# Attention, then two MLPs, on one core: four of the first MLP's sixteen FF chunks, instead of five, run along with the attention

## The chip, the core and the metric

One core of a Trainium2 chip runs the whole program. The metric is the device time of one execution in microseconds (us), as the median of several runs. TensorE (PE in the profile) multiplies, VectorE (DVE), ScalarE (ACT) and GpSimd (POOL) do the elementwise work, and SyncE's queue (SP) issues the DMAs. The weight loads of TensorE are listed as PEld.

## What is computed

Three stages follow one another on 4 x 576 = 2304 tokens. An attention with 8 heads of 64 (causal softmax, plus a memory term that is mixed in with a gate) gives x with 512 columns; the first MLP and the second MLP follow:

```python
a = softmax(causal(q @ k.T / 8)); local = a @ v
x = g * mem_out + (1 - g) * local              # (2304, 512)
h = x @ w_in                                   # w_in 512 x 2048
r = maximum(h, 0)
x = (s * (r * r) + b) @ w_out                  # w_out 2048 x 512
h = x @ w2_in; e = exp(h - h.max(-1))          # w2_in 512 x 1024
solu = h * e / e.sum(-1)
out = layernorm(solu) * g_ln @ w2_out          # w2_out 1024 x 512
```

All of it is float32 at the interface. The weights come as 64-bit numbers and are decoded on the chip.

## The kernel before, in words

A framework places the instructions: the program gives an order, a list scheduler with a simulated timeline puts the instructions on each engine's queue when it holds them to be ready, earlier program order first, and each engine then runs its queue strictly in that order. So an instruction can be put ahead of others that come before it in the program, unless an explicit edge (`tc.issue_after(ins)`, for instructions on the engine of `ins`) or a tile that isn't free yet holds it back.

**Precision.** Every matmul of the MLPs is a sum of three: the operands are split in a high and a low part, and high x high, high x low and low x high are added up in PSUM. `split_x` (L440) does this for x in 4 ACT and 4 DVE instructions (L442, L443).

**Weights.** `decode(n)` (L141) loads the n-th weight tile of a list `order` (512 KB, L147) and turns it into a high and a low float32 part: two ACT instructions (L152, L163), five DVE instructions (L153, L154, L156, L158, L164) and one POOL instruction (L159). `decode_to(n)` (L175) decodes up to the n-th tile; its ACT instructions are put behind the instruction in `mark`. Pool A holds RA tiles and pool B, which takes the attention's memory once that is free, RB; RA + RB is 25, and the list has 48 tiles.

**Attention.** `Attention` (L188) goes over 16 units (4 sequences x 4 pairs of heads). Each unit has five score steps, followed by transposes and the product with the values; the unit's part of x is written by L411. Sequence by sequence, x also goes to DRAM (`xd`, L414).

**First part of the first MLP.** The 2048 hidden columns are 16 chunks of 128. The first FP1 = 5 chunks are worked off sequence by sequence in `first_part` (L447), as a filler among the attention's instructions: for each half sequence of 288 tokens, FP1 hidden steps (`hidden`, L420: 12 matmuls of 288 columns, L424 to L426, then ACT L427, DVE L434, ACT L435, DVE L438) and 4 output steps (15 matmuls of 288 columns, L471 to L473, an ACT copy L475 and a store to `yd`, L477). Fillers start in the second sequence; a counter `debt` (L554) sets how many filler steps stand behind each score step. What is left when the attention has ended is worked off in a loop of its own (L567); there each step asks for one more weight tile, up to 25. This stretch is called the handoff here.

**Second part.** `second_part` (L571) takes the other FP2 = 11 chunks in two groups (5 and 6), each over five blocks of tokens (four of 512 and one of 256): a round is one group on one block. A round loads its block of x (L493), splits it, and does for each chunk a hidden step (12 matmuls, then four ACT instructions L427, L429, L430, L431 and one DVE, L432) and an output step (12 matmuls, L608 to L610). Four PSUM banks add up the round's outputs, which are added to `yT` (L638). The first round's split is put behind the last ACT copy of the first part (`lastact`, L588). Further weight tiles are decoded along the way.

**Second MLP.** `mlp2` (L685) goes over 18 tiles of 128 tokens. The first tile's softmax is begun in the last round, with its three statistics in three small tiles of their own (L630).

The lines that the change touches:

Of the kernel before, what the change touches and what calls it, by code (L numbers as in the profile page):

```python
# [8 lines left out]
F32 = mybir.dt.float32  # L9
# [8 lines left out]
P = 128  # L18
# [5 lines left out]
def attention_mlp_kernel(  # L24
# [9 lines left out]
    nc = tc.nc  # L34
# [60 lines left out]
        with nc.allow_non_contiguous_dma(reason="a small vector"):  # L95
            nc.sync.dma_start(gl_sb, g_ln.rearrange("(f p) -> p f", p=P))

    FP1 = 5
    FP2 = NF - FP1
    RA = 2 * FP1 + 8  # L100
    RB = 25 - RA
    assert 2 * FP2 <= RA + RB
    wpA = ctx.enter_context(tc.tile_pool(name="wpA", bufs=RA))
# [71 lines left out]
    def decode_to(n):  # L175
        while decoded[0] < min(n, NW):
            with tc.issue_after(mark[0]) if mark[0] else nullcontext():
                decode(decoded[0])
            decoded[0] += 1
# [235 lines left out]


    attended = [False]
    lastact = [None]

    def hidden(w, xh, xl, n, ps, r, gh, gl, square=False):  # L420

# [18 lines left out]
    def split_x(x, xh, xl):  # L440
        for c in range(NC):
            nc.scalar.activation(xh[:, c], x[:, c], AF.Copy)  # L442
            nc.vector.tensor_tensor(xl[:, c], x[:, c], xh[:, c].bitcast(F32), ALU.subtract)  # L443
# [3 lines left out]
    def first_part(b, pools):  # L447

        xs, gs, ys, _ = pools
        for sub in range(2):  # L450
            nm = f"{b}_{sub}"
            x = xbs[b][:, :, sub * N1:(sub + 1) * N1]
            xh = xs.tile([P, NC, N1], F32R, tag="xh", name=f"xh{nm}")
            xl = xs.tile([P, NC, N1], F32R, tag="xl", name=f"xl{nm}")
            split_x(x, xh, xl)
            gq = []
            for f in range(FP1):
                ps = pools[3][0].tile([P, 512], F32, tag="mh"[len(pools[3]) - 1], name=f"h{nm}_{f}")
                r = gs.tile([P, N1], F32, tag="r", name=f"r{nm}_{f}", bufs=2)
                g = gs.tile([P, 2, N1], F32R, tag="g", name=f"g{nm}_{f}")  # L460
                decode_to(f + 1)
                hidden(wtiles["in", f], xh, xl, N1, ps[:, 0:N1], r, g[:, 0], g[:, 1])
                gq.append(g)
                yield
            for c in range(NC):
                ps = pools[3][-1].tile([P, 512], F32, tag="m", name=f"y{nm}_{c}")
                o = ps[:, 0:N1]
                decode_to(2 * FP1)
                for f in range(FP1):
                    wc = [wtiles["out", f][:, t, c * P:(c + 1) * P] for t in range(2)]  # L470
                    nc.tensor.matmul(o, wc[0], gq[f][:, 0], start=(f == 0), stop=False)  # L471
                    nc.tensor.matmul(o, wc[1], gq[f][:, 0], start=False, stop=False)
                    nc.tensor.matmul(o, wc[0], gq[f][:, 1], start=False, stop=(f == FP1 - 1))  # L473
                y = ys.tile([P, N1], F32, tag="y", name=f"yo{nm}_{c}")
                lastact[0] = nc.scalar.activation(y, o, AF.Copy).ins  # L475
                t0 = b * S + sub * N1
                nc.sync.dma_start(yd[:, c, t0:t0 + N1], y)  # L477
                yield
# [19 lines left out]
    with ExitStack() as fctx:  # L498
        xp = fctx.enter_context(tc.tile_pool(name="xp", bufs=2))
        xs = fctx.enter_context(tc.tile_pool(name="xs", bufs=1))  # L500
        gs = fctx.enter_context(tc.tile_pool(name="gs", bufs=FP1 + 1))
        ys = fctx.enter_context(tc.tile_pool(name="ys", bufs=2))
        ps_m = fctx.enter_context(tc.tile_pool(name="ps_m", bufs=2, space=PSUM))
        fpools = [xs, gs, ys, [ps_m]]
        filler = []
        with ExitStack() as actx:
            at = Attention(actx, xp)
            NS = CF + 1
            G = NU * NS
            at.load(0, "kq")  # L510
            warm_up(16)
            load_gate()
            at.load(1, "kq")
            at.load(0, "q", "z", "v")
            at.phi(0)
            at.load(1, "q", "v")
            load_consts()
            LAG = 2
            FG = NPAIR * NS + LAG + 1
            debt = 0.0  # L520
            tiles_of = lambda i: (2 * i, 2 * i + 1) if i < CF else (2 * CF,)
            for g in range(G + LAG):
                u, i = divmod(g, NS)
                if g < G and i != 1:
                    at.scores(u, *((0, 1) if i == 0 else (i,)))
                if g < 4:
                    with tc.issue_after(at.last):
                        warm_up(6)
                if i == CF and u < NU:
                    at.load(u + 2, "kq")  # L530
                if i == 3 and u < NU:
                    at.load(u + 2, "q")
                    at.load(u + 1, "z")
                if i == 2 and 0 < u < NU:
                    at.phi(u)
                if i == 3 and u < NU:
                    at.gates(u)
                if i == CF and u < NU:
                    at.weigh(u)
                if 0 <= g - LAG:  # L540
                    lu, li = divmod(g - LAG, NS)
                    for t in tiles_of(li):
                        at.transposes(lu, t)
                    if li == CF - 1:
                        at.recip_t(lu)
                        at.phi_t(lu)
                    if li == CF:
                        at.values(lu)
                        at.load(lu + 2, "v")
                        if lu % NPAIR == NPAIR - 1:  # L550
                            filler.append(first_part(lu // NPAIR, fpools))
                decode_to(min(int(g / 3.4), RA))
                if filler and g >= FG:
                    debt += 0.93 * 6 * (FP1 + NC) / (G - FG)  # L554
                    while debt >= 1 and filler:
                        debt -= 1
                        if next(filler[0], 0) == 0:
                            filler.pop(0)
        wpools[1] = ctx.enter_context(tc.tile_pool(name="wpB", bufs=RB, side="right", reuse_waits="tile"))
        xs2 = pctx.enter_context(tc.tile_pool(name="xs2", bufs=1, side="right", reuse_waits="tile"))  # L560
        gs2 = pctx.enter_context(tc.tile_pool(name="gs2", bufs=2, side="right", reuse_waits="tile"))
        ps_y = pctx.enter_context(tc.tile_pool(name="ps_y", bufs=1, side="right", space=PSUM, reuse_waits="tile"))
        ps_h = pctx.enter_context(tc.tile_pool(name="ps_h", bufs=2, side="right", space=PSUM, reuse_waits="tile"))
        fpools[3] = [ps_h, ps_m]
        load2(0, False)
        attended[0] = True
        for it in filler:  # L567
            for _ in it:
                decode_to(min(decoded[0] + 1, RA + RB))

    def second_part():  # L571
        load2(0, True)
# [4 lines left out]
        for ri, (fs, bi) in enumerate(rounds):  # L577
# [7 lines left out]
            x = xq.pop(ri)  # L585
            xh = xs2.tile([P, NC, NB], F32R, tag="xh", name=f"xh2_{ri}")
            xl = xs2.tile([P, NC, NB], F32R, tag="xl", name=f"xl2_{ri}")
            with tc.issue_after(lastact[0]) if ri == 0 else nullcontext():  # L588
                split_x(x[:, :, 0:n], xh[:, :, 0:n], xl[:, :, 0:n])
            ys = [ps_y.tile([P, 512], F32, tag=f"y{c}", name=f"y2_{ri}_{c}") for c in range(NC)]  # L590
            gq = {}

# [19 lines left out]
            for i, f in enumerate(fs):  # L612
                hstep(f)
                if i >= 1:
                    ystep(fs[i - 1])
                step += 1
                if ri == 0:
                    decode_to(min(decoded[0] + 2, g2))
                elif ri < len(blocks):

                    decode_to(g2 + (late - g2) * step // steps)
                elif ri < last:

                    decode_to(late + (last2 - late) * step // steps)
                else:
                    decode_to(decoded[0] + 1)
                if ri == last and i == 2:

                    z = dec.tile([P, WN, 2], I32, tag="raw", name="z0").rearrange("p n t -> p (n t)").bitcast(F32)
                    first["z"] = weights_of(0, z, *(const.tile([P, 1], F32, name=f"t0_{k}") for k in range(3)))  # L630
            if ri == last:
                decode_to(NW)
                first[1] = products(1)
# [36 lines left out]
    def weights_of(t, z, mx, sm, mu):  # L670

        hh = products(t) if t not in first else first.pop(t)
        nc.vector.tensor_reduce(mx, hh, AX.X, ALU.max, negate=True)
        nc.scalar.activation(z, hh, AF.Exp, bias=mx, accum_out=sm)
        nc.vector.tensor_scalar(sm, sm, 1e-9, None, ALU.add)
        nc.vector.reciprocal(sm, sm)
        nc.vector.scalar_tensor_tensor(z, hh, sm, z, ALU.mult, ALU.mult, accum_out=mu)
        return z, mu
# [119 lines left out]
```

## Time and profile before

| | us |
|---|---|
| median of three runs | 884.39 |
| lowest and highest run | 883.9, 886.73 |
| the profiled execution | 885.48 |
| its span, first to last instruction | 883.7 |
| TensorE busy in it | 850.8 (96%) |
| VectorE, ScalarE, GpSimd busy in it | 539.9, 513.7, 182.8 |

The profile shows one execution. An engine's busy time is the union of its instructions; for TensorE the end of a matmul is modelled and overlaps the next one's start, so the rate of work is read from the distance of starts, not from durations. "Idle before" is the time an engine stood still ahead of an instruction, with the instruction that ended it.

### The profile page before, as it was taken

How to read it: one execution, taken by the hardware profiler on the slowest of the kernel's cores; microseconds unless marked ns; L12 is line 12 of the kernel's file. 1: busy time of each engine (PE TensorE's matmuls, PEld its weight loads, DVE VectorE, ACT ScalarE, POOL GpSimd, SP SyncE). 2: the span in 40 equal slices, each digit the busy share in tenths (PEclk: the TensorE clock that was granted, in tenths of full speed). 3: DMA queues.
4: the chain of work that ended last, by engine and by line, in shares of the span. 5: the costliest groups of instructions: out<-in, count | busy, mean ns of one | idle time of the engine just before them, and what ended most of it. 6: DMA issues, size and time to landing. Idle time of an engine off the chain costs nothing.

```text
span 883.7 us, 14245 instructions
## 1 busy us (share of the span) xinstructions
PE 850.8 (96%) x5344; PEld 699.0 (79%) x5344; DVE 539.9 (61%) x1236; ACT 513.7 (58%) x1094; POOL 182.8 (21%) x180
## 2 busy tenths in 40 slices
PE   7899889999999999899999999999999999999997
PEld 5677668888878878878888888888988888888885
DVE  3898986768778467922338864454775444454532
ACT  4776765666666665555558776556774333433332
POOL 4445351332333222200002311101120000000000
PEclk9999999999999999999999999999999999999999
DMA  7445242533343204472013422111200000000000
GB/s 228 133 148 184 79 155 59 155 97 119 115 149 118 69 1 156 147 263 95 3 45 114 144 100 96 48 48 55 89 24 1 25 25 23 13 24 24 25 25 36
DMA packets 41494, 76.44 MB, mean 86 GB/s; under 512 B 6352, under 2 KB 20176, under 8 KB 41424
## 3 DMA queue, kind: packets, MB, share of 16 engines
q1 hardware_dynamic: 41424, 75.52, 26.5%
q8 instruction: 42, 0.69, 0.3%
q14 instruction: 28, 0.23, 0.1%
HBM read 61.35 MB, written 14.16 MB: 85 GB/s over the span
## 4 chain that ended last, share of the span: by engine, by line
PE 78%; DVE 13%; ACT 3%; issue 2%; POOL 1%; DMA 1%; POOLq 0%; SPq 0%; ACTq 0%; DVEq 0%
PE h L424 7%; PE h L425 7%; PE h L426 7%; PE y L609 5%; PE y L608 5%; PE y L610 5%; PE h L665 4%; PE h L666 4%; PE h L667 4%; PE o L730 4%; PE o L729 4%; PE o L728 4%; PE pp L372 3%; PE s L315 3%; PE po L404 3%
## 5 line engine op out<-in xcount | busy, mean ns | idle before, releaser
L425 PE MATMUL h<-xl,w 128*128 128x512 f32 (+2 forms) x380 | 131.0, 345 | 2.1 <-DVE xl L443 2.1
L159 POOL TENSOR_TENSOR wa<-wa,raw 128x512 f32<-128x512 f32 x48 | 67.8, 1415 | 314.5 <-DVE raw L158 198.2
L424 PE MATMUL h<-xh,w 128*128 128x512 f32 (+2 forms) x380 | 130.0, 349 | 2.8 <-ACT xh L442 2.5
L426 PE MATMUL h<-xh,w 128*128 128x512 f32 (+2 forms) x380 | 129.2, 341 | 0.0
L427 ACT ACTIVATE r<-h 128x512 f32<-128x512 f32 (+2 forms) x95 | 45.6, 489 | 87.3 <-PE h L426 73.0
L298 ACT ACTIVATE pr<-pr,mx 128x128 f32<-128x128 f32 (+3 forms) x128 | 70.8, 555 | 37.5 <-DVE mx L331 37.5
L432 DVE TENSOR_TENSOR gl<-r,gh 128x512 fp32r<-128x512 f32 (+1 forms) x55 | 37.2, 685 | 88.1 <-ACT r L431 88.0
L424 PEld LDWEIGHTS h<-xh,w 128*128 128x128 f32 x380 | 70.9, 188 | 15.2 <-ACT xh L442 3.5
L425 PEld LDWEIGHTS h<-xl,w 128*128 128x128 f32 x380 | 71.5, 188 | 13.1 <-DVE xl L443 3.8
L608 PE MATMUL y<-gh,w 128*128 128x512 f32 (+1 forms) x220 | 80.8, 372 | 0.0
L609 PE MATMUL y<-gh,w 128*128 128x512 f32 (+1 forms) x220 | 80.8, 372 | 0.0
L426 PEld LDWEIGHTS h<-xh,w 128*128 128x128 f32 x380 | 71.5, 188 | 8.1 <-issue 0.4
L331 DVE CUSTOM_DVE_ANT_0 pr<-s,big 128x128 f32<-128x128 f32 (+3 forms) x128 | 56.2, 485 | 9.6 <-PE s L315 9.2
L375 ACT ACTIVATE pt<-pp 128x256 f32<-128x256 f32 (+2 forms) x96 | 47.2, 518 | 22.5 <-PE pp L372 22.0
L610 PE MATMUL y<-gl,w 128*128 128x512 f32 (+1 forms) x220 | 60.0, 372 | 0.0
L728 PE MATMUL o<-w,zh 128*128 128x512 f32 x144 | 56.8, 395 | 0.8 <-ACT zh L722 0.8
L730 PE MATMUL o<-w,zl 128*128 128x512 f32 x144 | 56.9, 395 | 0.6 <-DVE zl L723 0.6
L667 PE MATMUL h<-w,yl 128*128 128x512 f32 x144 | 56.6, 393 | 0.0
L729 PE MATMUL o<-w,zh 128*128 128x512 f32 x144 | 56.6, 393 | 0.0
L665 PE MATMUL h<-w,yh 128*128 128x512 f32 x144 | 56.6, 393 | 0.0
L666 PE MATMUL h<-w,yh 128*128 128x512 f32 x144 | 56.6, 393 | 0.0
L315 PEld LDWEIGHTS s<-kq 64*128 64x128 f32 x640 | 40.1, 187 | 19.3 <-issue 6.7
(142 smaller groups left out, 1959.1 us busy)
## 6 DMA issues: line engine op xcount, KB each, us to landing
raw<-in_moe_w_in_dram SPq DMA_DIRECT2D x24, 512.0 KB, 3.8
raw<-in_moe_w_out_dram SPq DMA_DIRECT2D x24, 512.0 KB, 3.5
kq<-in_kq_dram SPq DMA_DIRECT2D x16, 608.0 KB, 4.0
xr<-xd SPq DMA_DIRECT2D x8, 1024.0 KB, 5.9
q<-in_q_dram SPq DMA_DIRECT2D x16, 320.0 KB, 3.0
v<-in_v_dram SPq DMA_DIRECT2D x16, 320.0 KB, 3.1
xd<-xb SPq DMA_DIRECT2D x4, 1152.0 KB, 6.5
yd<-yo SPq DMA_DIRECT2D x32, 144.0 KB, 2.4
```

The lines of the kernel that those rows point to most:

```text
L424: nc.tensor.matmul(ps, wc[0], xh[:, c, 0:n], start=(c == 0), stop=False)
L425: nc.tensor.matmul(ps, wc[0], xl[:, c, 0:n], start=False, stop=False)
L426: nc.tensor.matmul(ps, wc[1], xh[:, c, 0:n], start=False, stop=(c == NC - 1))
L608: nc.tensor.matmul(o, wc[0], gh[:, 0:n], start=(f == fs[0]), stop=False)
L609: nc.tensor.matmul(o, wc[1], gh[:, 0:n], start=False, stop=False)
L610: nc.tensor.matmul(o, wc[0], gl[:, 0:n], start=False, stop=(f == fs[-1]))
L665: nc.tensor.matmul(o, yh[:, c], w[:, 0], start=(c == 0), stop=False)
L666: nc.tensor.matmul(o, yh[:, c], w[:, 1], start=False, stop=False)
L667: nc.tensor.matmul(o, yl[:, c], w[:, 0], start=False, stop=(c == NC - 1))
L728: nc.tensor.matmul(oo, zh, w[:, 0], start=(f == 0), stop=False)
L729: nc.tensor.matmul(oo, zh, w[:, 1], start=False, stop=False)
L730: nc.tensor.matmul(oo, zl, w[:, 0], start=False, stop=(f == NF2 - 1))
```

## The change

It moves one of the five chunks of the first part into the second, which then has twelve in two groups of six. It also drops the edge that holds the first round's split behind the last copy of the first part, lets the loop after the attention ask for a weight tile at every fourth step only (and the first rounds for the rest, evenly), and keeps the three statistics of the second MLP's first tile in columns of an older constant. Pool A keeps 18 tiles and pool B 7.

```diff
-    FP1 = 5
+    FP1 = 4
     FP2 = NF - FP1
-    RA = 2 * FP1 + 8
+    RA = 2 * FP1 + 10
     RB = 25 - RA
...
-    lastact = [None]
...
-                lastact[0] = nc.scalar.activation(y, o, AF.Copy).ins
+                nc.scalar.activation(y, o, AF.Copy)
...
         attended[0] = True
+        turn = 0
         for it in filler:
             for _ in it:
-                decode_to(min(decoded[0] + 1, RA + RB))
+                turn += 1
+                decode_to(min(decoded[0] + (turn % 4 == 0), RA + RB))
...
-            with tc.issue_after(lastact[0]) if ri == 0 else nullcontext():
-                split_x(x[:, :, 0:n], xh[:, :, 0:n], xl[:, :, 0:n])
+            split_x(x[:, :, 0:n], xh[:, :, 0:n], xl[:, :, 0:n])
...
                 if ri == 0:
-                    decode_to(min(decoded[0] + 2, g2))
+                    decode_to(decoded[0] + step % 2)
+                    early = decoded[0]
                 elif ri < len(blocks):
 
-                    decode_to(g2 + (late - g2) * step // steps)
+                    decode_to(early + (late - early) * step // steps)
...
-                    first["z"] = weights_of(0, z, *(const.tile([P, 1], F32, name=f"t0_{k}") for k in range(3)))
+                    first["z"] = weights_of(0, z, *(gate[:, k:k + 1] for k in range(3)))
```

## Rows read from the trace of the kernel before

**Rows 1.** Windows: stretch, us, PE, PEld, DVE, ACT, POOL busy, PEclk, DMA, GB/s.

```profile
119.00:322.70 203.70, 200.73 (x1696) 166.72 (x1695) 143.84 (x412) 133.00 (x349) 68.55 (x65) 1.00 0.35 108
...
337.10:384.50 47.40, 42.56 (x290) 39.94 (x290) 37.93 (x66) 24.33 (x57) 10.98 (x7) 0.96 0.52 161
384.50:676.00 291.50, 290.19 (x1375) 240.01 (x1376) 156.75 (x262) 186.96 (x315) 33.25 (x23) 1.00 0.25 82
```

**Rows 2.** Timeline, DVE: L411 ends units 1, 4, 6 and 15. Start, us.

```profile
29.05 0.69 DVE L411 TENSOR_TENSOR xb<-po,R 128x512 f32<-128x512 f32 x1
...
75.25 0.69 DVE L411 TENSOR_TENSOR xb<-po,R 128x512 f32<-128x512 f32 x1
...
119.02 0.69 DVE L411 TENSOR_TENSOR xb<-po,R 128x512 f32<-128x512 f32 x1
...
322.74 0.69 DVE L411 TENSOR_TENSOR xb<-po,R 128x512 f32<-128x512 f32 x1
```

**Rows 3.** Windows of L424 alone, then of L471 alone: stretch, us, PE busy.

```profile
119.00:322.70 203.70, 30.51 (x96) 17.96 (x96) 1.00 0.35 108
...
119.00:322.70 203.70, 31.49 (x102) 19.17 (x102) 1.00 0.35 108
```

**Rows 4.** Groups by line on PE from 337.1 to 384.5 us.

```profile
L471 PE MATMUL y<-g,w 128*128 128x288 f32 x52 | 16.0, 310 | 1.3 <-ACT g L435 1.1 <-ACT yo L475 0.3
...
L424 PE MATMUL h<-xh,w 128*128 128x288 f32 x44 | 13.0, 304 | 0.8 <-ACT xh L442 0.8
```

**Rows 5.** Timeline, PE: first and last of 18 back-to-back matmuls of 288 columns.

```profile
349.04 0.29 PE L471 MATMUL y<-g,w 128*128 128x288 f32 x1
...
351.29 0.29 PE L473 MATMUL y<-g,w 128*128 128x288 f32 x1
```

**Rows 6.** Timeline, PE: first and last of 23 back-to-back matmuls of 512 columns.

```profile
391.62 0.40 PE L425 MATMUL h<-xl,w 128*128 128x512 f32 x1
...
396.78 0.40 PE L426 MATMUL h<-xh,w 128*128 128x512 f32 x1
```

**Rows 7.** Timeline, PE, handoff: matmuls that waited, with the wait and what ended it.

```profile
357.78 0.40 PE L425 MATMUL h<-xl,w 128*128 128x288 f32 x1 [1.40 <-DVE xl L443]
...
374.52 0.53 PE L473 MATMUL y<-g,w 128*128 128x288 f32 x2 [0.42 <-DVE g L438]
376.12 0.52 PE L471 MATMUL y<-g,w 128*128 128x288 f32 x1 [1.07 <-ACT g L435]
...
379.56 0.43 PE L471 MATMUL y<-g,w 128*128 128x288 f32 x1 [0.26 <-ACT yo L475]
...
384.92 0.74 PE L424 MATMUL h<-xh,w 128*128 128x512 f32 x2 [1.07 <-ACT xh L442]
385.65 0.50 PE L425 MATMUL h<-xl,w 128*128 128x512 f32 x1
```

**Rows 8.** Windows, all engines (columns as in rows 1).

```profile
376.00:378.00 2.00, 1.88 (x8) 1.88 (x9) 1.39 (x3) 0.50 (x2) 0.00 (x0) 0.56 0.52 199
```

**Rows 9.** Groups by line on DVE from 337.1 to 384.5 us.

```profile
L438 DVE SCALAR_TENSOR_TENSOR g<-r,b_sb,g 128x288 fp32r<-128x288 f32 x11 | 8.6, 795 | 0.0
L434 DVE SCALAR_TENSOR_TENSOR r<-r,s_sb 128x288 f32<-128x288 f32 x11 | 6.5, 605 | 1.9 <-ACT r L427 1.9
...
L443 DVE TENSOR_TENSOR xl<-xb,xh 128x288 fp32r<-128x288 f32 x8 | 3.2, 447 | 0.0
```

**Rows 10.** The tile xr, 330 to 380 us: the first round's load, and its landing.

```profile
L493 SPq DMA_DIRECT2D xr<-xd x1: 567/567/567, 337.5 to 337.5; - x1
...
DMA to landing us min/median/max: 6.9/6.9/6.9
```

**Rows 11.** Groups by line and form, whole span: decode and split on ACT and DVE.

```profile
L152 ACT ACTIVATE wa<-raw 128x512 f32<-128x512 f32 x48 | 31.5, 664 | 3.0 <-DVE w L164 1.6 <-DMA raw<-in_moe_w_in_dram 1.4
...
L163 ACT ACTIVATE w<-wa 128x512 fp32r<-128x512 f32 x40 | 24.9, 625 | 12.2 <-POOL wa L159 12.2
...
L443 DVE TENSOR_TENSOR xl<-xr,xh 128x512 fp32r<-128x512 f32 x32 | 22.4, 749 | 19.0 <-ACT xh L442 19.0
```

## The prediction, made before the changed kernel was run

> **What bounds the kernel now.** I first read the windows by stage, because the share of TensorE over the whole span (96%) hides four stages with different limits. From 384.5 to 676 us (the second part) TensorE is busy for 290.2 of 291.5 us, with VectorE at 156.8 and ScalarE at 187.0: this stage is TensorE's own work, and the other two engines have a third to a half of it free [rows 1]. From 119 to 322.7 us (attention with fillers) it is busy for 200.7 of 203.7, but VectorE for 143.8 and ScalarE for 133.0. From 337.1 to 384.5 us (the handoff, when no attention is left to fill gaps) TensorE is busy for only 42.6 of 47.4 us, and VectorE for 37.9.
>
> A busy TensorE need not be at its peak, so the second view is the pace of the attention. L411 writes each unit's result: from the 1st to the 4th unit, almost without fillers, 46.2 us pass, 15.4 per unit; from the 6th to the 15th 203.7 us pass, 22.6 per unit [rows 2]. In that second stretch L424 runs 96 times and L471 102 times [rows 3]; their two sister lines run as often, so there are 594 filler matmuls, 66 per unit. Each therefore lengthened the attention by 7.2 / 66 = 0.11 us. Back to back, such a matmul costs (351.29 - 349.04) / 17 = 0.132 us [rows 5]. So the attention is paced by the fillers on TensorE: that is the point on which the forecast turns.
>
> The third view is the handoff's waits. L471 and L424 run 52 and 44 times there [rows 4], with their sisters 288 matmuls, 38.0 us at 0.132; the stretch is 47.4, so 9.4 us are lost. The timeline shows where: 1.40 us for a split on VectorE, 0.42 and 1.07 for the squares of the last hidden steps, 0.26 for a copy, and 1.07 for the first round's split [rows 7]. Behind the pair of waits at 374 and 376 us the granted clock is 0.56 of full speed [rows 8], so most of that window was at the lower of the two levels (1.2 against 2.4 GHz); 14 matmuls take the 3.44 us from 376.12 to 379.56 [rows 7] instead of 1.85, 1.6 more.
>
> **The change part by part.** *The moved chunk, out of the first part.* The first part falls from 960 to 768 matmuls of 288 columns (24 per chunk and half sequence, 8 half sequences). How many leave the attention follows from the counter: it adds 0.93 x 6 x 9 / 57 = 0.88 steps per score step now, 0.84 after, over 59 of them, so 51 filler calls become 49. Now the program leaves 312 matmuls for the handoff and the trace has 288, so 24 were pulled ahead; after, the program leaves 12 + 192 = 204. I take 198. The attention then loses 672 - 570 = 102 matmuls, the handoff 90.
>
> In the attention, a matmul is worth 0.11 us by the pace [rows 2, 3] and 0.132 back to back [rows 5]: 11.2 to 13.5 us. The pace is the nearer row, but its base, the first units, also holds the start-up; I take 0.12, **-12.2 us**. The bound on the other side is nothing at all (a rival, below). In the handoff, 90 x 0.132 = **-11.9 us**.
>
> *The moved chunk, into the second part.* A chunk is 24 matmuls per block. One of 512 columns costs (396.78 - 391.62) / 22 = 0.2345 us [rows 6], one of 256 by the same rate 0.117. So 24 x (4 x 0.2345 + 0.117) = **+25.3 us**, all on the path, since this stage has no idle TensorE. Its five more hidden steps on ScalarE and VectorE lie under TensorE [rows 1]; if that cover were gone, a round would wait at its end. The work itself is thus nearly moved at par: -24.1 against +25.3, +1.2.
>
> *Fewer decodes in the handoff.* Now the loop asks for seven tiles in its first seven steps; after, for four in seventeen steps, the last of them behind the last hidden step. VectorE's 37.9 us there are 15.1 for 11 hidden steps (1.37 each), 3.2 for splits [rows 9], and so 19.6 for seven decodes, 2.8 each. After, until the last hidden step is squared, there are 8 x 1.37 + 3.2 + 3 x 2.8 = 22.6 us, 15.3 fewer. The rest of the stretch, 9.5 us, is a start and a last row of output steps, which have 48 matmuls instead of 60, 1.6 us. Handoff by this reckoning: 47.4 - 16.9 = 30.5 us, against 198 x 0.132 = 26.1 of work; the loss falls from 9.4 to 4.4, 5.0 less.
>
> *The unordered split.* The first round's x is ready long before it is used: its load is issued at 337.5 us and lands 6.9 us later [rows 10], while the matmul that needs it waits until 384.92 [rows 7]. Without the edge, the split can be done earlier, and hidden steps of the first round can stand in TensorE's gaps. What surely goes is the gap of 1.07 us and some 0.4 of the ragged start behind it (385.65 - 384.92 for two matmuls). What it adds: 4 x 0.749 = 3.0 us on VectorE [rows 11] at a time when that engine is the late one. Taken together with the decodes, the bounds are 2 us (the split takes back on VectorE what the decodes free) and 9.8 (no loss is left, 9.4 + 0.4); I take **-6 us**, nearest to the sum of the two reckonings, 6.5.
>
> *Three tiles later.* The three decodes that the handoff loses go to the first round (at every other step), the other rounds have theirs evenly. Each is 0.664 + 0.625 us on ScalarE [rows 11] and some 2.8 on VectorE per 11 us of TensorE work (two steps of 24 matmuls): covered [rows 1]. The tiles are not needed early: 22 are there when the second part starts, and the first group uses the first 20. SP issues these loads later too, among the loads of x and yT; nothing waits for them for a round.
>
> *The statistics in an old constant:* the five instructions of that softmax follow one another already, and the constant's last reader is long gone. Nothing.
>
> Sum: -12.2 - 11.9 + 25.3 - 6 = **-4.8 us**. The profiled execution took 885.5, which gives 880.7; the median, 884.4, is 1.1 lower, so 879.6.
>
> **A rule against it.** The pace of the attention says that a filler taken out gives back 0.11 us [rows 2, 3], so that it costs there nearly what it costs elsewhere. The Trainium skill (Perfetto Trace Analysis, Optimization Strategy) says that a kernel whose busiest engine changes from stage to stage may gain by interleaving the stages; this change takes work out of such an interleaving, and by the rule's strict form the chunk was free under the attention. The pace so far speaks against that form; what it would make of the time is rival 2.
>
> **The rivals.** *1, the loss in the handoff stays.* The split's ACT instructions may be put ahead of where x has landed: 337.5 + 6.9 is 7.3 us behind the attention's end. ScalarE's queue then stands, the next relu of a filler behind it, and TensorE runs dry as soon as two PSUM banks are full (24 matmuls, 3.2 us): up to 4 us, and again a stretch at the lower clock, 1.6. Or VectorE, with the split's 3.0 us more, stays as late as now. Either takes 4 to 6 us of the 6: 884 to 885. For it: VectorE is busy for 80% of the handoff [rows 1]. Against it: it has 15 us less to do.
>
> *2, slower: the attention gives nothing back.* If its own chain (scores, minimum on VectorE, exp on ScalarE, transposes) sets the end at 337.1 us, the -12.2 is lost: 879.6 + 12.2 = 891.8. It decides from 4.8 us on: the attention has to give back 7.4 us, 0.073 per matmul, for a gain. Against it: 15.4 us per unit with few fillers, when 21.5 is all that is asked after the change; TensorE idle for 3.0 of 203.7 us [rows 1]. For it: a list scheduler places everything anew, and VectorE is at 71%.
>
> *3, the change does not do what it says:* the split, last in program order, still finds VectorE full and comes after the last fillers. Then only the decodes' 5.0 us are won: 880.6, inside the forecast's range.
>
> **How the numbers follow.** The forecast has a chance of 0.54, rival 3 of 0.1, rival 1 of 0.2, rival 2 of 0.1, and 0.06 is left for a stage that is reordered in a way that I don't see. The forecast's own range is 874.5 (13.5 and 9.8 instead of 12.2 and 6: 5.1 less) to 884.6 (11.2 and 2: 5.0 more). A measurement can tell 0.3% here, 2.7 us: faster is under 881.7, slower over 887.1. Of the 0.64 of the forecast and rival 3, 0.6 lies under 881.7 and 0.04 within; rival 1 puts 0.16 within and 0.02 on either side; rival 2 puts 0.08 over and 0.02 within; the rest is split evenly. That makes 0.64 faster, 0.24 the same, 0.12 slower. The range reaches from the forecast's low end, 874.5, over rival 1 to 887, and leaves out the upper half of rival 2 and part of the rest.
>
> **What would show it.** In the changed profile: the attention's last matmul near 325 us instead of 337; about 285 each of L471 to L473 and L424 to L426 together before it (570); a handoff of 27 to 31 us up to the first L608; L442 on xr before the last L475, and 512-column L424 among the last 288-column ones; no stretch at half clock there; each round of the first group about 5.6 us longer. Wrong would be: an attention that still ends after 333 us (rival 2), or a wait of L442 on the load of xr with relus behind it, or VectorE waits of over 1 us left in the handoff (rival 1).

## The result, and the profile after

The changed kernel takes 869.31 us (869.15 to 870.64), the kernel before 884.89 beside it; the ratio is 0.9825, with a 95% interval from 0.9805 to 0.9844: 15.6 us less. The forecast was 879.6 in a range from 874.5 to 887, so the sign was right, and the time lies 5 us below the range. The profiled execution took 869.15 us, its span is 867.4 instead of 883.7.

The windows by stage of the changed kernel, to be read beside [rows 1] (columns as there):

```profile
113.50:304.60 191.10, 187.57 (x1593) 151.49 (x1592) 144.47 (x410) 130.57 (x347) 68.74 (x65) 1.00 0.37 115
322.20:361.60 39.40, 36.12 (x230) 34.14 (x231) 31.55 (x54) 24.34 (x50) 7.91 (x6) 0.96 0.55 173
361.60:659.80 298.20, 298.20 (x1453) 252.83 (x1452) 154.71 (x263) 192.68 (x325) 32.79 (x24) 1.00 0.25 81
659.80:867.40 207.60, 202.14 (x962) 167.94 (x961) 99.40 (x191) 79.27 (x138) 10.34 (x18) 1.00 0.06 23
```

The first line is the attention from the 6th to the 15th unit: 191.1 us where it was 203.7 [rows 1, 2]. The attention's last matmul starts at 322.2 us instead of 337.1, 14.9 us earlier. From there on the kernel takes 545.2 us (867.4 - 322.2) instead of 546.6: nothing but 1.4 us less, although one chunk more is computed in it. And the last line is a surprise: the second MLP, of which the change moves no instruction, is shorter. The same window of the kernel before, from the last L610 to the end, was 1.9 us longer:

```profile
674.20:883.70 209.50, 203.82 (x962) 168.05 (x960) 99.28 (x191) 79.26 (x138) 10.32 (x18) 0.99 0.06 23
```

The matmul counts are equal (962), so the same matmuls run faster. The next view is a window of 40 us in which every matmul has 512 columns, TensorE alone, first before, then after:

```profile
400.00:440.00 40.00, 40.00 (x173) 1.00 0.09 31
```

```profile
400.00:440.00 40.00, 40.00 (x178) 1.00 0.13 40
```

TensorE is busy all the time in both, at the full clock, yet 178 matmuls fit where 173 did. The timeline of the changed kernel shows the steady beat, to be read beside [rows 6] (first and last of 23):

```profile
399.82 0.39 PE L610 MATMUL y<-gl,w 128*128 128x512 f32 x1
...
404.81 0.39 PE L608 MATMUL y<-gh,w 128*128 128x512 f32 x1
```

(404.81 - 399.82) / 22 = 0.2268 us, against 0.2345 before. Over the whole second part, the mean distance of back-to-back starts of 512 columns is 226.8 ns after and 232.2 before. There it jumps, and with the pool that holds the weights: matmuls with weights from pool B start 228 ns apart, those with weights from pool A 234, most of these between 230 and 238.

In the handoff, one wait of TensorE is new. First the timeline of PE and of ACT, then a window of all engines:

```profile
332.59 0.59 PE L470 MATMUL y<-g,w 128*128 128x288 f32 x1 [3.05 <-ACT g L434]
...
346.99 0.39 PE L423 MATMUL h<-xh,w 128*128 128x512 f32 x1
```

```profile
329.92 2.19 ACT L441 ACTIVATE xh<-xr 128x512 fp32r<-128x512 f32 x4 [3.59 <-DMA xr<-xd]
```

```profile
334.00:336.00 2.00, 2.00 (x10) 2.00 (x10) 2.00 (x6) 1.01 (x4) 0.00 (x0) 0.50 0.65 165
```

The split (L441 after, L442 before) was put so early that ScalarE stood for 3.59 us until x had landed and then did the split's four instructions (2.19 us) ahead of the instruction that the fillers needed (L434, which writes their hidden tile g). TensorE waited 3.05 us for it; behind that the granted clock is 0.50 of full speed, the lower level, and 14 filler matmuls take the 3.51 us from 332.59 to 336.10 instead of 1.86 (0.1325 each), so 1.65 more. Later, 29 hidden and 8 output matmuls of 512 columns of the first round stand among the last fillers, from 346.99 on.

### The profile page after: what moved, and what is told of

It is laid out like the page before. It is cut to its first block, busy times and chain, and to the rows that moved or that the text cites. A ratio compares the mean times of both kernels' runs of the same rounds, so it can differ in the third digit from the quotient of the medians.

```text
span 867.4 us, 14074 instructions
## 1 busy us (share of the span) xinstructions
PE 840.6 (97%) x5272; PEld 694.8 (80%) x5272; DVE 532.2 (61%) x1225; ACT 518.4 (60%) x1098; POOL 179.8 (21%) x180
## 3 DMA queue, kind: packets, MB, share of 16 engines
q1 hardware_dynamic: 41424, 75.52, 27.1%
## 4 chain that ended last, share of the span: by engine, by line
PE 81%; DVE 8%; ACT 5%; POOL 2%; issue 2%; DMA 2%; POOLq 0%; SPq 0%; ACTq 0%; DVEq 0%
PE h L423 7%; PE h L424 7%; PE h L425 7%; PE y L609 6%; PE y L608 6%; PE y L610 6%; PE h L668 4%; PE h L666 4%; PE h L667 4%; PE po L404 4%; PE o L731 4%; PE o L730 4%; PE o L729 4%; PE pp L372 3%; PE s L315 3%; PE y L470 2%
## 5 line engine op out<-in xcount | busy, mean ns | idle before, releaser
L159 POOL TENSOR_TENSOR wa<-wa,raw 128x512 f32<-128x512 f32 x48 | 65.4, 1362 | 322.7 <-DVE raw L158 232.6
L424 PE MATMUL h<-xl,w 128*128 128x512 f32 (+2 forms) x368 | 128.5, 350 | 0.0
L423 PE MATMUL h<-xh,w 128*128 128x512 f32 (+2 forms) x368 | 126.3, 350 | 1.1 <-ACT xh L441 0.9
L425 PE MATMUL h<-xh,w 128*128 128x512 f32 (+2 forms) x368 | 125.9, 343 | 0.0
L431 DVE TENSOR_TENSOR gl<-r,gh 128x512 fp32r<-128x512 f32 (+1 forms) x60 | 39.8, 667 | 85.3 <-ACT r L430 84.9
L609 PE MATMUL y<-gh,w 128*128 128x512 f32 (+1 forms) x240 | 87.4, 368 | 0.0
L608 PE MATMUL y<-gh,w 128*128 128x512 f32 (+1 forms) x240 | 87.3, 368 | 0.0
L423 PEld LDWEIGHTS h<-xh,w 128*128 128x128 f32 x368 | 68.8, 189 | 11.8 <-ACT xh L441 1.6
L424 PEld LDWEIGHTS h<-xl,w 128*128 128x128 f32 x368 | 69.5, 189 | 9.4 <-issue 1.2
L425 PEld LDWEIGHTS h<-xh,w 128*128 128x128 f32 x368 | 69.4, 189 | 8.4 <-issue 0.9
L610 PE MATMUL y<-gl,w 128*128 128x512 f32 (+1 forms) x240 | 64.6, 368 | 0.0
L331 DVE CUSTOM_DVE_ANT_0 pr<-s,big 128x128 f32<-128x128 f32 (+3 forms) x128 | 56.0, 483 | 12.2 <-PE s L315 11.6
L429 ACT ACTIVATE gh<-r,b_sb,s_sb 128x512 fp32r<-128x512 f32 (+1 forms) x60 | 45.7, 770 | 18.8 <-PE y L609 18.0
```

Source lines behind the costliest of these rows:

```text
L423: nc.tensor.matmul(ps, wc[0], xh[:, c, 0:n], start=(c == 0), stop=False)
L424: nc.tensor.matmul(ps, wc[0], xl[:, c, 0:n], start=False, stop=False)
L425: nc.tensor.matmul(ps, wc[1], xh[:, c, 0:n], start=False, stop=(c == NC - 1))
L608: nc.tensor.matmul(o, wc[0], gh[:, 0:n], start=(f == fs[0]), stop=False)
L609: nc.tensor.matmul(o, wc[1], gh[:, 0:n], start=False, stop=False)
L610: nc.tensor.matmul(o, wc[0], gl[:, 0:n], start=False, stop=(f == fs[-1]))
```

## The experiments

Theory A arose from the second MLP: the pace of a matmul depends on where its two tiles lie. In the built program, dropping three constants of 32 bytes each moved every later tile of the memory's left side (pool A, the second MLP's tiles) by 96 bytes; the right side (pool B, and x and the hidden tiles of the second part) stayed. The rival, B, was that the new order, or less work on the other engines, made the difference.

**1 and 2: the constants alone, taken back and done alone.** The edit of run 1; run 2 is its reverse on the kernel before:

```diff
-                    first["z"] = weights_of(0, z, *(gate[:, k:k + 1] for k in range(3)))
+                    first["z"] = weights_of(0, z, *(const.tile([P, 1], F32, name=f"t0_{k}") for k in range(3)))
```

> The changed kernel with the three statistics back in three constants of their own, which moves every later tile on that side of the memory by 96 bytes. Theory A (placement: back-to-back matmuls of 512 columns start every 227 ns when the weight tile and the moving tile begin at the same place within 64 bytes, every 234 ns when not): pool A's weights and the moving tiles of the second part are apart again, so the mean distance of starts in the second part goes from 226.8 to about 232 ns, 1152 x 5.5 ns = 6.3 us more there (less 0.5 for the 256-column ones), and some 2 us more in the second MLP: 869.3 + 7.8 = 877. Theory B (the shorter distance comes from the new order of the instructions, or from less work beside them on the other engines): nothing changes, 869.3, and the distance stays at 226.8 ns.

> The kernel before, with the three statistics in columns of the old constant and nothing else. Theory A: the distance of starts falls from 232 to 227 ns in the second part (1056 x 5.5 = 5.8 us, less 0.4) and the second MLP is 2 us shorter, while the attention still ends at 337 us and the handoff keeps its waits: 884.9 - 7.4 = 877.5. Theory B: 884.9, distance 232 ns.

Measured: run 1 877.40 us, ratio to the kernel before 0.9930 (0.9905 to 0.9955); run 2 877.08, 0.9923 (0.9902 to 0.9944). The distance of starts is back at 232.4 ns in run 1 and falls to 226.9 in run 2. The 40 us window, first run 1, then run 2:

```profile
400.00:440.00 40.00, 40.00 (x173) 1.00 0.13 40
```

```profile
400.00:440.00 40.00, 40.00 (x178) 1.00 0.12 38
```

Run 2 has the old order of the handoff, with its waits and its half-clock stretch, and still its matmuls keep the new beat, and the second MLP is 207.9 us long; run 1 has the new order, and the old beat. B falls. The place alone is worth 6.3 us in the kernel before (883.41 beside run 2) and 8.1 in the changed one (877.40 against 869.31, on another chip). In run 2 the attention ends at 335.3 us instead of 337.1; no experiment explains these 1.8 us, and among the placements of the changed kernel its end scatters by as much, from 321.2 to 323.0.

**3, 4, 10, 13 and 14: which place.** One unused constant ahead of pool A, of 32, 64, 128, 256 and 512 bytes (here run 3's):

```diff
+    const.tile([P, 8], F32, name="pad")
     warm = const.tile([P, 256], mybir.dt.bfloat16, name="warm")
```

> The changed kernel with one unused constant of 32 bytes ahead of pool A, so that pool A's weights begin at another place within 64 bytes than the second part's moving tiles. Theory A: the second part is slow as in the kernel before (mean 232 ns), the second MLP partly: about 877. If only three extra tiles, or the statistics' own place, mattered: 869.3.

> The same with 64 bytes: the same place within 64 bytes as the moving tiles, but another one within 128. Theory A with 64 as the unit: as the changed kernel, 869.3 and 226.8 ns. Theory A with 128 as the unit: about 877 and 232 ns. Theory B: 869.3.

> The changed kernel with 128 unused bytes ahead of pool A. If 128 bytes are the unit of the placement: as the changed kernel, distance 227 ns, 869.3. If a larger unit decides: about 877 and 232 ns, as with 64 bytes.

> The changed kernel with 256 unused bytes ahead of pool A. If 256 bytes are the unit of the placement: distance 227 ns and 869 to 871. If it is 512 or more: about 232 ns and 877.

> The same with 512 bytes. If 256 or 512 bytes are the unit: 227 ns and 869 to 871. If it is larger: about 232 ns and 877.

**15: the moving tiles instead of the weights.** A spare pool of 32 bytes on the right side, so that x and the hidden tiles of the second part move and nothing else:

```diff
+        padr = pctx.enter_context(tc.tile_pool(name="padr", bufs=1, side="right", reuse_waits="tile"))
+        padr.tile([P, 8], F32, name="pad")
         xs2 = pctx.enter_context(tc.tile_pool(name="xs2", bufs=1, side="right", reuse_waits="tile"))
```

> The changed kernel with 32 unused bytes beside the second part's moving tiles, so that these alone move (x and the hidden tiles of the second part); all weight tiles and the whole second MLP stay where they are. If the pair decides (weight tile against moving tile): all 512-column matmuls of the second part, those with pool B's weights too, go to about 234 ns, 1152 x 7.7 ns = 8.9 us more, less 0.5 for the 256-column ones, and the second MLP stays at 207.5 us: 878. If the place of the left side alone decides: 869 to 871, 227 ns.

All placements in one table. The columns A, B and moving are the tile's address modulo 256 in the built program (pool A's and pool B's weights, the second part's moving tiles). In the second MLP the roles are exchanged: the decoded weights of pools A and B are its moving tiles, and the tiles that they are multiplied with lie on the left side and have A's value. "Distance" is the mean distance of starts in the second part. Each ratio is to the kernel before beside that run, on the same chip, so that it is not the quotient of two medians of the table.

| kernel | A | B | moving | distance, ns | second MLP, us | median, us | ratio to before |
|---|---|---|---|---|---|---|---|
| before | 64 | 224 | 224 | 232.2 | 209.5 | 884.89 | 1 |
| changed | 224 | 224 | 224 | 226.8 | 207.5 | 869.31 | 0.9825 |
| 1 | 64 | 224 | 224 | 232.4 | 209.2 | 877.40 | 0.9930 |
| 2 | 224 | 224 | 224 | 226.9 | 207.9 | 877.08 | 0.9923 |
| 3, 32 bytes | 0 | 224 | 224 | 231.9 | 209.2 | 877.86 | 0.9930 |
| 4, 64 bytes | 32 | 224 | 224 | 232.0 | 209.3 | 875.68 | 0.9907 |
| 10, 128 bytes | 96 | 224 | 224 | 231.5 | 209.1 | 877.02 | 0.9914 |
| 13, 256 bytes | 224 | 224 | 224 | 226.9 | 207.6 | 870.33 | 0.9850 |
| 14, 512 bytes | 224 | 224 | 224 | 226.8 | 207.6 | 870.84 | 0.9851 |
| 15 | 224 | 224 | 192 | 233.3 | 207.5 | 876.49 | 0.9920 |

Run 4 refuted theory A's unit of 64 bytes, and run 10 the 128 that run 4 had left; 13 and 14 gave 256. So pool A was tried at 32, 64, 96 and 128 bytes from the moving tiles, and all are slow; other distances weren't tried. Run 15 shows that the pair decides: all weights lie as in the changed kernel, only the moving tiles don't, and the second part is slow, with pool B's weights too (233.3 ns, where the kernel before has 228), while the second MLP, whose pairs still agree, keeps its 207.5 us. The length of the second MLP is a sign only at the full clock: in run 11 below, the changed kernel once more, it is 209.2 us with the same places and a distance of starts of 226.8 ns in the second part, because the granted clock is 0.94 from 840 us to the end. The 40 us window of run 15:

```profile
400.00:440.00 40.00, 40.00 (x173) 1.00 0.12 40
```

**5: five chunks again.**

```diff
-    FP1 = 4
+    FP1 = 5
     FP2 = NF - FP1
-    RA = 2 * FP1 + 10
+    RA = 2 * FP1 + 8
```

> The changed kernel with five chunks again in the first part (pool A keeps 18 tiles); placement, unordered split and even decode as changed. Theory C (the chunk is worth what its matmuls cost on either side): against the changed kernel the attention ends 14.9 us later (near 337), the handoff has 96 more matmuls of 288 columns, 12.7 us, and the second part is 96 x 0.2267 + 24 x 0.1197 = 24.6 us shorter: 869.3 + 3.0 = 872.3. Theory D (the moved chunk gives nothing; all that the placement leaves comes from the handoff): 869.3. Theory E (the moved chunk gives all that the placement leaves): about 877.

Measured 872.68 us, 0.9869 (0.9847 to 0.9891). The attention's last matmul is at 337.2 us, so the 14.9 us of the attention are the chunk's, and the sum of C is hit: the chunk by itself is worth about 3 us here. That size is a rough one, since run 5's four executions lie between 869.81 and 873.96.

**6 and 7: the split, and the decoding, taken back one at a time.** Run 6 (the edge back), then run 7 (the old pace):

```diff
+    lastact = [None]
...
-                nc.scalar.activation(y, o, AF.Copy)
+                lastact[0] = nc.scalar.activation(y, o, AF.Copy).ins
...
-            split_x(x[:, :, 0:n], xh[:, :, 0:n], xl[:, :, 0:n])
+            with tc.issue_after(lastact[0]) if ri == 0 else nullcontext():
+                split_x(x[:, :, 0:n], xh[:, :, 0:n], xl[:, :, 0:n])
```

```diff
-                decode_to(min(decoded[0] + (turn % 4 == 0), RA + RB))
+                decode_to(min(decoded[0] + 1, RA + RB))
...
-                    decode_to(decoded[0] + step % 2)
-                    early = decoded[0]
+                    decode_to(min(decoded[0] + 2, g2))
...
-                    decode_to(early + (late - early) * step // steps)
+                    decode_to(g2 + (late - g2) * step // steps)
```

> The changed kernel with the first round's split behind the last copy again. Theory F (the unordered split costs as much as it gives): the wait of 3.05 us for a split whose x has not landed and the half-clock stretch behind it, 1.3 us, go, while the gap ahead of the first round, some 1.5 us, and waits of some 4 us that first-round matmuls fill now come back: 868 to 871, the same as the changed kernel. Theory G (the unordered split is worth the loss of the handoff): 4 us or more slower, over 873.

> The changed kernel with the old pace of decoding: one tile at every step of the loop behind the attention, up to 25, and the first rounds' old targets. By the reckoning of the prediction VectorE gets 3 x 2.8 = 8.4 us more in the handoff, and TensorE waits for 5 us of it: 874. If matmuls of the first round fill those waits: at most 2 us slower, 869 to 871.

Measured: run 6 868.14 us, 0.9824 (0.9809 to 0.9839); run 7 869.51, 0.9837 (0.9822 to 0.9852). Neither can be told from the changed kernel. In run 6 the attention's end and the last filler are 27.1 us apart for 25.4 us of fillers (192 at 0.1325), with no wait above 0.4 us, and then the gap ahead of the first round is there again, 1.1 us. In run 7 more of the first round's matmuls (51 instead of 37) fill the handoff. My reckoning of 5 us for three decodes does not show there: VectorE's lateness is covered by work of the next stage.

**9: both taken back at once.** The kernel before with the edits of the chunk and of the constants alone.

> The kernel before with the moved chunk and the statistics in the old constant alone: the split is behind the last copy and the old pace of decoding is back, both at once. Theory I (the split's freedom and the slower decoding each cure the same waits in the handoff, so that undoing one of them cost nothing): undoing both brings some 4 us back, 872 to 875. Theory J (with four chunks the handoff needs neither): 868 to 870, as the changed kernel.

Measured 877.48 us, 0.9922 (0.9899 to 0.9945): 8 us over the changed kernel, the direction of I with twice its size, and no better than the placement alone (run 2). The waits of TensorE from 321.8 to 380 us (in total, times, longest), and two windows:

```profile
PE h L424 <- ACT xh L442: 2.4, 1, 2.4
PE y L471 <- ACT g L435: 1.5, 1, 1.5
PE h L424 <- DVE xb L411: 1.1, 1, 1.1
PE y L473 <- DVE g L438: 0.6, 1, 0.6
```

```profile
348.00:350.00 2.00, 2.00 (x9) 2.00 (x10) 2.00 (x5) 0.34 (x1) 0.00 (x0) 0.52 0.88 305
358.00:360.00 2.00, 1.56 (x4) 1.23 (x5) 1.58 (x3) 1.94 (x4) 0.00 (x0) 0.58 1.02 373
```

The gap ahead of the first round is 2.4 us instead of 1.07 [rows 7], and the lower clock comes back at both places. Run 9 differs from run 6 by the pace of decoding alone and from run 7 by the split's edge alone, so these three and the changed kernel are the four combinations of the two edits, with the same chunk and the same places: both edits 869.31, decoding alone (run 6) 868.14, split alone (run 7) 869.51, neither 877.48. The split's freedom and the slower decoding cure the same waits: either is enough, without both the chunk's gain is lost. Where the 8 us lie shows best against run 6, whose profile is 10.9 us shorter. The handoff from the attention's last matmul to the last filler, first in run 9, then in run 6:

```profile
321.80:355.70 33.90, 30.07 (x193) 28.80 (x193) 29.24 (x51) 17.03 (x38) 11.91 (x7) 0.90 0.57 193
321.40:348.60 27.20, 26.57 (x194) 25.84 (x194) 22.32 (x42) 14.97 (x35) 5.36 (x4) 1.00 0.55 174
```

That is 6.7 us of the 10.9, for the same 192 fillers: VectorE has 6.9 us more to do, and TensorE's mean granted clock is 0.90 instead of 1.00. Of the rest, 2.2 us lie in the second part and 1.6 in the second MLP, where run 9's granted clock is 0.99 and run 6's 1.00.

**8, 11 and 12: the split behind an earlier instruction.** The changed kernel stands on x's load; so let the split wait for the first output copy of the last sequence's first half:

```diff
+    lastact = [None]
...
-                nc.scalar.activation(y, o, AF.Copy)
+                copied = nc.scalar.activation(y, o, AF.Copy).ins
+                if sub == 0 and c == 0:
+                    lastact[0] = copied
...
-            split_x(x[:, :, 0:n], xh[:, :, 0:n], xl[:, :, 0:n])
+            with tc.issue_after(lastact[0]) if ri == 0 else nullcontext():
+                split_x(x[:, :, 0:n], xh[:, :, 0:n], xl[:, :, 0:n])
```

> The changed kernel with the first round's split behind an earlier instruction: the first copy of the last sequence's first half (its first output step) instead of no edge. By then x has landed, so ScalarE does not stand in front of relus. Theory H (the wait of 3.05 us and the half-clock stretch of 1.3 us behind it are a loss of the unordered split): both go and first-round matmuls still fill gaps: 865. Rival (the wait only moves to another place, VectorE being late anyway): 868 to 870.

> The changed kernel itself, for a comparison on the same chip with the next: 868 to 870.

> The version with the first round's split behind the first copy of the last sequence's first half, again: 864 to 866, 4 us under the changed kernel, if the earlier gain was no chance of the chip.

Measured: run 8 865.16 us, 0.9783 (0.9765 to 0.9801); then on one chip run 11, the changed kernel again, 870.57, 0.9838 (0.9814 to 0.9861), and run 12, the same as run 8, 864.67, 0.9773 (0.9752 to 0.9794). This version beats both kernels: 19 to 20 us under the one before, 4 to 6 under the changed one (6 on one chip). Its handoff in run 8's profile, and TensorE's waits in run 12 from 322 to 380 us:

```profile
323.60:358.30 34.70, 34.44 (x230) 32.51 (x231) 30.40 (x54) 24.17 (x50) 7.42 (x6) 1.00 0.62 197
```

```profile
PE h L424 <- ACT r L427: 0.2, 1, 0.2
```

As many matmuls as in the changed kernel's handoff (230, the second line of the first fence) take 34.7 us instead of 39.4, with 0.2 us of waits and at the full clock.

## Why the prediction was wrong

| step | forecast, us | measured in the profiles, us |
|---|---|---|
| fewer fillers under the attention | -12.2 | -14.9 |
| fewer fillers in the handoff | -11.9 | -12.7 (96 x 0.1325) |
| the chunk in the second part, at the old pace | +25.3 | +25.1 (96 x 0.2322 + 24 x 0.118) |
| waits and half clock from the attention's end to the end of the second part | -6 | -6.1 (11.6 to 5.5) |
| the statistics in an old constant | 0 | -7.8 (-5.8 in the second part, -2.0 in the second MLP) |
| sum | -4.8 | -16.4 |

**The step that failed** is the shortest one: "The statistics in an old constant ... Nothing." I priced the five instructions and the wait they might have, and not where the allocator puts everything behind three tiles of 32 bytes. It is half of the gain: 8.1 of 15.6 us by run 1, which puts only these three tiles back and takes 877.40 us, inside the range. The trace of before held the sign of it: the distances of the 512-column starts there fall in two groups, near 227 and from 231 to 238 ns, and I took 0.2345 from one stretch [rows 6] as the matmul's price.

**The attention** gave back 14.9 us instead of 12.2: 96 matmuls left it (102 forecast), 0.155 us each, over my upper bound of 0.132. Between the 6th and the 15th unit the pace was as I read it: 477 fillers instead of 594, 12.6 us less, 0.108 each. The last unit has 28 fillers where it had none, and is 3.3 us longer, 0.12 each. What I missed is the sixth unit. It holds 12 filler matmuls in either kernel, and is 22.0 us long before and 17.6 after (first line before, second after):

```profile
97.03:119.02 21.99, 17.15 (x162) 12.53 (x160) 20.56 (x53) 15.36 (x41) 8.31 (x8) 1.00 0.30 97
95.88:113.47 17.59, 15.59 (x142) 11.56 (x144) 14.86 (x45) 12.47 (x32) 8.08 (x8) 1.00 0.41 133
```

VectorE is busy for 20.6 of the 22.0 us there and TensorE for 17.2, so in this unit the attention was not "paced by the fillers on TensorE", as the prediction has it: VectorE had 5.7 us less to do, and 4.4 came back. Before, a split (L443, 3.0 us) and some 3 us more of decoding stand in it. Run 5 shows that all of the 14.9 us comes with the chunk; that VectorE is what set the sixth unit is read from the two profiles alone, and no experiment takes its work there away.

That 96 lies so near to 102 is luck. With four chunks the counter adds 0.93 x 6 x 8 / 57 = 0.78 per score step and not 0.84, which makes 46 filler calls instead of 49. The program then leaves 240 matmuls for the handoff, and 48 of them were pulled ahead, where I had 204 and 6.

**The chunk at par** was right: +25.1 against -27.6, and run 5's 3 us.

**The handoff** was right in its sum and wrong in its reckoning; that -6 and -6.1 agree is luck. I expected less lateness on VectorE and a saved gap; what came is a new wait on x, the mechanism of rival 1 (up to 4 us and a half-clock stretch of 1.6 forecast, 3.05 and 1.65 measured), which first-round matmuls in the rest of the handoff paid for. Runs 8 and 12 show the wait's price, 4 to 6 us. Runs 6, 7 and 9 show that the two edits aren't terms that add up: with the split behind the last copy, the slower decoding is worth about 9 us (run 9 against run 6; 5.0 forecast), with the split free nothing (run 7).

**Rival 2** fell with the attention's end at 322 us, and with it the strict form of the rule that the prediction sets against its forecast; **rival 3** fell too, since the split stands before the last fillers.

## What to carry to other kernels

A tile added, dropped or resized moves all tiles behind it, so compare the distance of starts of unchanged matmuls before anything else; a change in a stage that the diff does not touch is the sign. Where float32r matmuls (fp32r, the type that the splits write) of 512 columns are the bound, try the weight tile and the moving tile at the same address modulo 256, and pad for it. An instruction that is freed from an edge may need another one, just late enough that its data has landed; here ScalarE's strictly ordered queue stood in front of it.

## What the runs showed of the hardware

With the weight tile and the moving tile at the same address modulo 256, back-to-back float32r matmuls of 512 columns start every 226.8 ns, otherwise every 232.6 to 234.1 on average; in the table six kernels with pool A or the moving tiles apart and four with all at one value agree, and the kernel before shows both at once (228 ns with pool B's weights, 234 with pool A's, in the same rounds). Agreement at 64 or at 0 serves as well as at 224 (the second MLP's first product, with pool A's weights, keeps 227.4 ns in the kernel before and in run 3). The Trainium skill (TensorE: Matmul & The Clock Gate, "Step-by-step: what each phase is for") says that the two operands come through separate read ports, so that loading the next weights takes nothing from the running matmul. Of an effect of the two tiles' addresses that section says nothing, and the table shows one: their relative place costs some 3% of the matmul's time. Whether the weight loads take it or something else, the runs do not show. For the 256-column matmuls of the second part it is the other way round, 119.8 ns at the same place and 118.1 apart. The 288-column fillers were not moved against their weights, but in every kernel each second slice of their x lies 128 bytes from its weights and the others at the same place: 133 against 132 ns in the kernel before, hardly a difference.
